# First loads on one queue, a small extra read of the modulation weights, and the last store on another engine

## The chip, the core and the metric

The kernel runs on one core of one Trainium2 chip. The core has five engines with instruction queues of their own: TensorE (PE in the profile; its weight loads are listed apart as PEld), VectorE (DVE), ScalarE (ACT), GpSimd (POOL) and SyncE (SP), which here only issues transfers. Transfers run on 16 DMA engines that all queues share. Transfers issued by SyncE appear as queue q1 in the profile, those issued by ScalarE as q10. The metric is device time in microseconds (us) of one execution, given as the median of several runs.

## What is computed

A transformer block with adaptive layer norm: a condition vector c gives six modulation rows, a local dilated attention (32 heads of 16, a window of 8 positions with a step of 2) is added to x, and then a token-mixing MLP over the 2048 positions. B = 1, S = 2048, D = 512, F = 1792; all inputs are bfloat16.

```python
mod = (silu(c) @ w_mod).reshape(1, 6, 1, 512)        # w_mod: 512 x 3072
sa, ca, ga, sb, cb, gb = (mod[:, i] for i in range(6))
h = layernorm(x) * (1 + ca) + sa
x = x + ga * A(h, wqkv, wo)                          # local dilated attention
h = layernorm(x) * (1 + cb) + sb
x = x + gb * B(h, w1, b1, w2, b2)                    # B normalizes again, then
# u = gelu(einsum('bsd,sf->bdf', h, w1) + b1);  y = einsum('bdf,fs->bds', u, w2) + b2;  transposed back
```

## The kernel before, in words

**How the order is made.** The kernel first builds a graph of named operations, each with the engines it may run on and what it reads and writes. A long string, `ORDER`, lists all the names in the order in which they are emitted; `name:2` gives a PSUM slot (there are four, `ps0` to `ps3`) and `name:v`, `name:a` or `name:g` the engine. `schedule` checks that nothing comes before what it depends on. Each engine then runs its own operations in that order. Places of operations of different engines relative to each other have no meaning beyond their data. Since all operations are recorded through one helper, the profile gives line 184 for nearly everything, and tiles must be used to tell them apart.

**How transfers are issued.** `dma` (line 346) issues on SyncE unless told `"act"`. Completion is counted on eight counters that are used in turn by all transfers, in the order in which they are emitted: a transfer's issue waits until the transfer eight places earlier, which had the same counter, has landed. SyncE runs its issues strictly in order, so a waiting issue holds those behind it.

**The start.** x has 2048 rows in 16 tiles of 128 (`xx`), in four chunks of four tiles. The transfers are named: `ld_c` (c, ScalarE), `ld_x00` and `ld_x02` (tiles 0, 1 and 2, 3 of chunk 0, 256 KB each), `ld_wmodA` and `ld_wmodB` (the first 1024 columns of `w_mod`, its upper and lower 256 rows, 512 KB each, into tile `vD0`; called wmodA and wmodB below), `ld_w1a`, `ld_w1b` (the key weights `w_k`, 256 KB each), `ld_x1a`, `ld_x1b`, `ld_x2`, `ld_x3` (the other chunks), `ld_w0` (`w_q`), `ld_w2` (`w_v`), then the other modulation weights (`ld_wmod5` and so on, into `wst`) and `woq`. Before the change SyncE issues x00, x02, wmodB, w1a, x1a, w1b, x1b, x2, w0, w2, x3 in this order, and ScalarE issues c and then wmodA, ahead of its table load.

The first computations of chunk 0 are: `cps` and the silu of c (ScalarE and VectorE, `silu_exp`, `silu_dve`), the statistics `ln1s0` to `ln1s3` of the four tiles (VectorE takes 0, 2 and 3, ScalarE takes 1), `rstd1_0_0` and `rstd1_0_2` on ScalarE, the normalization `ln1n0` to `ln1n3` into `n_sb` on VectorE, 16 transposes on TensorE in four groups (`tr0_00`, `tr0_10`, `tr0_02`, `tr0_12`), and the modulation columns. For these, `modcols0` (from wmodA) and `modcols1` (from wmodB) are 16 products each with one column; `modcols_h` copies the first half (`mchalf`), and `modcols_cp` adds the second half, into `sacol` and `a1col`. With these, `hT0_0` to `hT0_3` scale and shift the transposed tiles: ScalarE does `hT0_0`, VectorE the other three. Then come the projections, keys first: `qkvk0_0` (its second half, `qkvk0_0b`, needs all of hT), `qkvk0_2`, `qkvk0_1`, then the queries (`qkvq0_...`, from `w_q`). `warm0` to `warm4` are products of a constant with itself whose result is never read; `WARM` gives their counts. `warm4` stands between the last transposes and `qkvk0_0`.

**What follows.** For each chunk: products of q and k on VectorE (`qk`, 128 x 4096), their reduction on TensorE (`red`), softmax, products with the shifted v (`pv`, VectorE; `pvacc`, TensorE), the output projection (`wo`), two more normalizations (`t`, `aff`, `h3`). The first MLP product runs in two halves (`mlp1_0_...` over the positions of chunks 0 and 1, `mlp1_1_...` over the others), joined by `gadd`, `gelu` and `gbm`. The second MLP product (`mlp2_...`) runs over 16 tiles of output rows; `fin` adds the residual on VectorE, and `st_out` stores. Tile 15 is split into columns 0 to 383 and 384 to 511; its second part, `st_out15_384`, is the last store, right behind `st_out14_0` on SyncE.

Of the kernel before, what the change touches and what calls it, by code (L numbers as in the profile page):

```python
# [32 lines left out]
qkvq0_2:3 ln1n7:v evk0_2:a evq0_0:a rstd1_2_0 qk0_1 evq0_2:a tr1_10:2 tr1_00:1 ld_w2 ld_x3 ld_wmod5 ld_wmod3 ld_wo0
ld_wmod2 ld_wo2 ld_wo1 khalo1 ld_wmod4 qkvv0_0:0 qk0_0 hT1_0:a hT1_1:a hT1_2:a hT1_3:a qk0_3 qk0_2 evv0_0:a qkvv0_2:3
qkvq1_0:1 evv0_2:a ln1s14:a vd0_111 vd0_010 vd0_031 vd0_100 vd0_101 vd0_021 vd0_030 vd0_001 vd0_020 vd0_011 vd0_000
vd0_130 vd0_120 vhalo1 evq1_0:a nb1_2_0 qkvk1_0:2 red0_0:0 evk1_0:a red0_1 ln1s12:v ln1s13:v ln1n11:g ln1n10:g red0_2
red0_3 qk1_1 qkvq1_2:3 ln1s15:a rstd1_3_0 ln1n8:a evq1_2:a ln1n9:a qkvk1_2:1 max0 qk1_0 sub0 qkvv1_0:2 evk1_2:a exp0
tr2_10:3 evv1_0:a sum0 rb0 tr2_00:1 qkvv1_2:2 hT2_1:a qk1_3 smul0 qk1_2 nb1_3_0 khalo2 vd0_110 vd0_131 vd0_121 hT2_0:a
hT2_3:a a2_0:0 a2ev0:a red1_0:3 modrows:0 pv0_0 pv0_1 hT2_2:a ln1n14:a evv1_2:a mrow_ev ln1n12:a ln1n13:a ln1n15:a
qkvq2_0:1 red1_1 red1_2 red1_3 pvacc0_0:2 max1 pvacc0_1 evq2_0:a tr3_00:0 pv0_2 pv0_3 sub1 hT3_0:a vd1_011 vd1_020  # L40
ld_wo3 bc0 vd1_031 qkvk2_0:1 exp1 vd1_010 vd1_030 vd1_000 vd1_021 vd1_001 sum1 hT3_2:a oev0_1:a qkvv2_0:0 rb1 evk2_0:a
smul1 pvacc0_2:2 evv2_0:a vd1_130 vd1_110 vd1_120 vd1_100 vd1_101 vd1_111 vd1_131 vd1_121 pvacc0_3 gmul a2_1:3
oev0_3:a tr3_10:1 qk2_1 hT3_1:a a2ev1:a wo3:0 wo0:2 wo2:3 x1ev3:a hT3_3:a x1ev0:a x1ev2:a x1sq0 wo1:0 pv1_0 pv1_1
qkvq2_2:1 pvacc1_0:2 qk2_0 x1ev1:a x1sq3 x1sq2 x1sq1 pvacc1_1 qkvv2_2:3 qkvk2_2:0 rstd2_0_0 evq2_2:a nb2_0_0 pv1_2
qkvq3_0:1 t1:a t3:a t2:v pv1_3 oev1_1:a evk2_2:a evq3_0:a t0:a bc3 bc1 bc2 ld_w1_0_0 vhalo2 khalo3 ld_w1_0_2 ld_b2
ld_w1_0_3 pvacc1_2:2 red2_0:0 qk2_3 pvacc1_3 qkvk3_0:1 oev1_3:a evv2_2:a aff0_0 wo6:2 evk3_0:a wo4:3 x1ev6:a vd2_110
vd2_001 vhalo3 vd2_031 ld_b1 vd2_120 ld_w1_0_1 vd2_000 wo5:1 qk2_2 x1sq6 x1ev4:a wo7:2 x1sq4 x1ev5:a red2_1 ln3s0_1:v
x1ev7:a qk3_1 x1sq5 x1sq7 qkvk3_2:3 red2_2 rstd2_1_0 red2_3 evk3_2:a nb2_1_0 qkvq3_2:1 t5:a t7:g t6:g t4:g ln3s0_3:a
ln3s0_2:v max2 ln3s0_0:v sub2 qkvv3_2:2 exp2 rstd3_0_0 evq3_2:a biascols:3 sum2 qkvv3_0:1 aff1_0 nb3_0_0 evv3_2:a
h3_0:a h3_1:g h3_2:g ln3s1_1:a rb2 ln3s1_0:a evv3_0:a ln3s1_3:v biascols_cp ln3s1_2:v h3_3:v qk3_0 smul2 qk3_2  # L50
mlp1_0_30_0:3 mlp1_0_10_0:2 mlp1_0_31_0 a2_2:0 mlp1_0_11_0 rstd3_1_0 vd2_021 vd2_111 vd2_030 vd2_020 vd2_011 vd2_121
ld_w1_0_6 vd2_010 vd2_131 vd2_130 vd3_020 vd3_030 vd3_010 vd2_100 a2ev2:a red3_0:1 red3_1 nb3_1_0 qk3_3 red3_2
mlp1_0_00_0:0 mlp1_0_01_0 h3_4:v h3_5:a h3_6:a h3_7:a red3_3 pv2_0 mlp1_0_11_4 mlp1_0_31_4 mlp1_0_10_4 mlp1_0_01_4
max3 park0_1:a pv2_1 sub3 pvacc2_0:2 exp3 mlp1_0_30_4 pv2_2 vd2_101 vd3_000 vd3_031 vd3_001 vd3_011 vd3_110 vd3_021
vd3_121 vd3_100 vd3_120 vd3_130 ld_w1_0_4 vd3_131 vd3_111 vd3_101 sum3 mlp1_0_00_4 pvacc2_1 park0_3:a rb3 oev2_1:a
smul3 mlp1_0_60_0:3 pv2_3 a2_3:1 mlp1_0_61_0 pvacc2_2:2 a2ev3:a pvacc2_3 pv3_0 mlp1_0_60_4 mlp1_0_61_4 oev2_3:a wo10:1
wo8:2 pv3_1 park0_6:a x1ev10:a x1sq10 park0_0:a wo11:3 x1ev8:v wo9:1 x1ev11:v pvacc3_0:2 ld_w1_1_0 ld_w1_0_5 ld_w1_1_1
ld_w2_4 ld_w1_1_5 ld_w1_1_3 x1ev9:v pvacc3_1 pv3_2 mlp1_0_20_0:0 mlp1_0_21_0 mlp1_0_40_0:3 mlp1_0_21_4 mlp1_0_20_4
mlp1_0_40_4 pvacc3_2:1 x1sq8 x1sq11 x1sq9 rstd2_2_0 nb2_2_0 pv3_3 t8:v t10:a t9:a t11:a aff2_0 pvacc3_3 oev3_1:a
park0_2:a oev3_3:a ln3s2_3:a ln3s2_1:v ln3s2_2:v ln3s2_0:v mlp1_0_41_0 mlp1_0_41_4 wo12:2 wo13:0 park0_4:a x1ev12:v  # L60
rstd3_2_0 wo14:1 wo15:3 mlp1_0_50_0:2 x1ev13:v x1sq12 nb3_2_0 x1sq13 h3_8:a rstd2_3_0 x1ev14:v x1ev15:v h3_10:g
h3_11:g mlp1_0_51_0 mlp1_0_51_4 mlp1_0_50_4 h3_9:v nb2_3_0 t13:v t12:v x1sq15 x1sq14 aff3_0 rstd2_3_2 park0_5:a
# [5 lines left out]
mlp1_1_41_4 gelu5 gelu4 gbm7 gadd5 gbm5 gbm6 gbm2 gelu10 gelu11 gbm10 gadd4 gbm4 gbm11 mlp1_1_60_0:2 mlp1_1_61_0
mlp1_1_61_4 mlp1_1_60_4 gelu8 gelu9 gbm8 gbm9 mlp2_3_0_0:3 mlp2_1_0_0:0 gadd6 gelu13 gelu12 xb3 gbm12 gbm13
mlp2_3_12_0 mlp2_2_0_0:1 fin3_0 xb2 st_out3_0 xb0 xb1 mlp2_2_12_0 xb7 mlp2_0_0_0:2 fin2_0 st_out2_0 ld_w2_2  # L70
mlp2_1_12_0 mlp2_0_12_0 mlp2_7_0_0:3 fin0_0 mlp2_7_12_0 mlp2_6_0_0:1 fin7_0 xb6 st_out7_0 st_out0_0 mlp2_6_12_0
mlp2_11_0_0:2 fin6_0 xb4 st_out6_0 ld_w2_7 mlp2_5_0_0:3 xb10 xb11 fin1_0 st_out1_0 mlp2_10_0_0:1 xb5 mlp2_11_12_0
# [894 lines left out]
```

## Time and profile before

| what | value |
|---|---|
| median of 3 runs | 198.81 us (198.49 to 199.16) |
| the profiled execution: its own time | 198.58 us |
| its span, first to last instruction | 196.4 us |
| TensorE busy | 190.3 us (97%), 1290 products |
| VectorE busy | 154.3 us (79%) |
| ScalarE busy | 124.0 us (63%) |
| GpSimd busy | 11.9 us (6%) |
| moved by DMA | 33.58 MB, of it 32.85 MB on SyncE's queue and 0.53 MB on ScalarE's |

The profile shows one execution. Its 2.2 us beyond the span lie before the first and after the last instruction. Busy shares are averages over stages: TensorE's products are pipelined and their ends are modelled, so 97% doesn't mean that it ran at its peak. In the profile's 40 slices each digit is a busy share in tenths for 4.9 us. In its timeline a line is: start (us from the span's start), duration, engine, operation, tiles written and read, shape, count, and in brackets the idle time before it and what ended it. In the chain of waits a line is: start, duration, what. In the list of transfers the last figure is the time from issue to landing in us. The trace also has a record of every DMA packet (start, duration, size and queue); where a number comes from there, the text says packet records.

### The profile page before, as it was taken

What the parts mean: (1) busy time and instruction counts of PE and PEld (TensorE: products, weight loads), DVE (VectorE), ACT (ScalarE), POOL (GpSimd) and SP (SyncE); (2) the same over time, 40 slices, a digit from 0 to 9 for tenths busy, and PEclk for the clock granted to TensorE, in tenths of its full rate; (3) what the DMA queues carried; (4) which work ended last, traced back from release to release, by engine and by line L of the source; (5) the groups of instructions that cost most, each with busy time, mean ns of one, the idle gap of its engine ahead of it and who ended that gap; (6) DMA issues with size and microseconds to landing.
All of it is one profiled execution on the core that took longest, in us unless ns stands there. A gap on an engine that the chain in (4) does not pass through costs nothing.

```text
span 196.4 us, 3401 instructions
## 1 busy us (share of the span) xinstructions
PE 190.3 (97%) x1290; PEld 88.8 (45%) x1290; DVE 154.3 (79%) x200; ACT 124.0 (63%) x241; POOL 11.9 (6%) x41
## 2 busy tenths in 40 slices
PE   7999999899999999999999999999999999999994
...
DVE  1799999999999999999999998827984547142463
...
PEclk9999999999999999999999999999999999999999
DMA  6999999346990995299599989999000164511112
GB/s 195 364 348 326 244 189 167 94 137 157 158 232 11 239 230 164 76 222 190 130 217 290 292 240 292 291 294 243 3 0 0 57 201 129 150 44 36 57 57 76
DMA packets 45347, 33.58 MB, mean 171 GB/s; under 512 B 5396, under 2 KB 42772, under 8 KB 45332
## 3 DMA queue, kind: packets, MB, share of 16 engines
q1 hardware_dynamic: 45052, 32.85, 67.5%
q10 hardware_dynamic: 280, 0.53, 0.8%
q8 instruction: 10, 0.16, 0.4%
...
## 4 chain that ended last, share of the span: by engine, by line
PE 58%; ACT 23%; DVE 11%; issue 5%; DMA 2%; SPq 0%; DVEq 0%; ACTq 0%
PE ps L184 58%; ACT junk L184 4%; ACT hTb L184 3%; DVE pvb L184 3%; ACT n_sb L184 2%; ACT v_c L184 2%; ACT q_sb L184 2%; DMA xx<-in_A_x_dram 2%; ACT k_c L184 2%; DVE prod L184 2%; DVE st L184 2%; DVE h L184 2%; ACT xx L184 1%; ACT a2sb L184 1%; ACT ee L184 1%
## 5 line engine op out<-in xcount | busy, mean ns | idle before, releaser
L184 DVE TENSOR_TENSOR pvb<-a2sb,vD 128x4096 bf16<-128x4096 bf16 x16 | 36.2, 2289 | 0.4 <-issue 0.2
L184 PE MATMUL ps<-h,wst 128*128 128x512 bf16 x128 | 29.3, 380 | 0.0
L184 DVE TENSOR_TENSOR prod<-q_sb,k_c 128x4096 bf16<-128x4096 bf16 x9 | 20.6, 2296 | 0.1
L184 PE MATMUL ps<-gT,vD 128*128 128x512 bf16 x84 | 19.1, 379 | 0.0
L184 PEld LDWEIGHTS <-wst 128*128 128x128 bf16 x128 | 12.1, 98 | 15.5 <-issue 1.7
L184 DVE TENSOR_TENSOR k_c<-ps,k_c 128x512 bf16<-128x512 f32 (+2 forms) x9 | 5.6, 630 | 13.4 <-PE ps L184 13.4
L184 PE MATMUL ps<-woq,o_sb 128*128 128x512 bf16 x64 | 15.7, 379 | 0.0
L184 PE MATMUL ps<-hTb,w_v 128*128 128x512 bf16 x64 | 15.0, 380 | 0.4 <-ACT q_sb L184 0.4
L184 PEld LDWEIGHTS <-w_q 128*128 128x128 bf16 x96 | 10.1, 109 | 11.2 <-issue 1.7
L184 PE MATMUL ps<-hTb,w_q 128*128 128x512 bf16 x64 | 15.0, 381 | 0.0
L184 PE MATMUL ps<-hTb,w_k 128*128 128x512 bf16 x64 | 15.0, 380 | 0.0
L184 PEld LDWEIGHTS <-o_sb 128*128 128x128 bf16 x106 | 9.7, 98 | 10.3 <-ACT o_sb L184 0.4
L184 DVE TENSOR_TENSOR q_sb<-ps,q_sb 128x512 bf16<-128x512 f32 x8 | 5.4, 687 | 11.1 <-PE ps L184 11.1
L184 PEld LDWEIGHTS <-vD 128*128 128x128 bf16 x116 | 9.3, 97 | 10.1
L184 PE MATMUL ps<-gT,pvb 128*128 128x512 bf16 x56 | 12.9, 379 | 0.0
L184 PEld LDWEIGHTS <-w_k 128*128 128x128 bf16 x80 | 8.7, 111 | 8.9 <-issue 0.8
L184 PE MATMUL ps<-gT,prod 128*128 128x512 bf16 x56 | 12.2, 379 | 0.0
L184 PEld LDWEIGHTS <-w_v 128*128 128x128 bf16 x80 | 8.3, 110 | 8.6 <-issue 1.7
L184 ACT ACTIVATE junk<-xx,su 128x512 bf16<-128x512 bf16 x16 | 11.6, 726 | 0.3
L184 DVE BATCH_NORM_STATS2 st<-xx 128x6 f32<-128x512 bf16 x11 | 7.4, 674 | 4.6 <-DMA xx<-in_A_x_dram 4.6
L184 ACT ACTIVATE gT<-n_sb,b1col 128x512 bf16<-128x512 f32 x8 | 5.4, 714 | 8.8 <-DVE n_sb L184 8.8
L184 ACT ACTIVATE hTb<-ps,sacol,a1col 128x512 bf16<-128x512 bf16 x13 | 9.6, 780 | 1.4 <-PE ps L184 1.4
(111 smaller groups left out, 315.6 us busy)
## 6 DMA issues: line engine op xcount, KB each, us to landing
...
wst<-in_B_w_dram SPq DMA_DIRECT2D x8, 512.0 KB, 6.2
...
wst<-in_w_mod_dram SPq DMA_DIRECT2D x4, 512.0 KB, 9.4
...
xx<-in_A_x_dram SPq DMA_DIRECT2D x4, 256.0 KB, 3.5
xx<-in_A_x_dram SPq DMA_DIRECT2D x2, 512.0 KB, 8.0
```

The source lines that it names most:

```text
L184: r = fn(*a, **k)
```

## The change

Five things are changed in the code:

- `ld_wmodA` is issued by SyncE, as third transfer, between `ld_x02` and `ld_wmodB`. The rest of the order of SyncE's first loads stays.
- A new transfer, `ld_touch`, takes its place on ScalarE: it reads the first 32 columns (64 B) of rows 0, 8, 16, ... 504 of `w_mod` into a tile of 64 x 32 that nothing reads.
- The last store, `st_out15_384`, is issued by ScalarE.
- The last count in `WARM` is 5, not 6.
- `ORDER` is written anew. Engine by engine, this changes little beyond the above. TensorE: `modcols1` now stands ahead of all the transposes (before: behind `tr0_00`); in the second half of the first MLP product, `mlp1_1_00_0` stands ahead of `mlp1_1_11_0`, `mlp1_1_20_4` ahead of `mlp1_1_50_4`, and `mlp1_1_41_4` ahead of `mlp1_1_40_4`. VectorE: `modcols_h` ahead of `ln1n3`; `t8` ahead of `pv3_3`; `gadd5` ahead of `gbm7`. SyncE: `ld_w2_0` (into `prod0`) goes behind `ld_w1_1_4`, `ld_w2_5` and `ld_w2_3`. GpSimd: nothing.

Since the touch is one more transfer at the start, the transfers behind it use the next counter: the issue of `ld_w1b` now waits for c, `ld_x1b` for x00, `ld_x2` for the touch, `ld_w0` for x02, `ld_w2` for wmodA and `ld_x3` for wmodB (before: `ld_x1b` for c, `ld_x2` for x00, and the others as now).

```diff
 ORDER = """
-consts ld_c ld_x00 consts2 warm0:0 ld_x02 ld_wmodA act_table ld_wmodB ld_w1a ld_x1a cps:1 warm1:2 ld_w1b silu_exp
-ln1s0:v ld_x1b ln1s1:a ld_x2 silu_dve halo0 ld_w0 warm2:3 ln1s2:v rstd1_0_0 ln1s3:v modcols0:0 nb1_0_0 ln1n0:v warm3:1
-rstd1_0_2 ln1n1:v nb1_0_2 ln1n2:v tr0_00:2 ln1n3:v modcols1 modcols_h tr0_10:3 tr0_02 modcols_cp tr0_12 sc_rep hT0_1:v
+consts ld_c ld_x00 consts2 warm0:0 ld_touch ld_x02 act_table ld_wmodA ld_wmodB ld_w1a cps:1 warm1:2 ld_x1a silu_exp
+ln1s0:v ld_w1b ln1s1:a ld_x1b silu_dve ln1s2:v halo0 ld_x2 warm2:3 ld_w0 ln1s3:v rstd1_0_0 modcols0:0 rstd1_0_2 ld_w2
+nb1_0_0 ln1n0:v warm3:1 ln1n1:v nb1_0_2 ln1n2:v modcols1 modcols_h ln1n3:v ld_x3 tr0_00:2 tr0_10:3 modcols_cp tr0_02
...
-    WARM=(4, 4, 4, 4, 6),
+    WARM=(4, 4, 4, 4, 5),
...
+    touch = T([D // 8, 32], BF, "touch")
...
     dma(c_t[:], c[0].rearrange("(t p) -> t p", p=P), 1024, [], ["c_t"], "ld_c", "act")
+    dma(touch[:], w_mod.rearrange("(a b) n -> a b n", b=8)[:, 0, 0:32], 4096, [], ["touch"], "ld_touch", "act")
...
-    dma(wmodA[:, 0:2, :], wmod_view[:, 0:2, 0:2 * D], 2 * D * P * 2 * 2, [], vdk[0][4:], "ld_wmodA", "act")
+    dma(wmodA[:, 0:2, :], wmod_view[:, 0:2, 0:2 * D], 2 * D * P * 2 * 2, [], vdk[0][4:], "ld_wmodA")
...
                 dma(out_flat[st * P:(st + 1) * P, c0:c1], ostage[:, c0:c1], P * nc_ * 2, ok[1:] or ok, [("out", st, c0)],
-                    f"st_out{st}_{c0}")
+                    f"st_out{st}_{c0}", "act" if st == NST - 1 and c1 == D else "sp")
```

More of the change, by code (lines that the diff above doesn't have):

```diff
@@ L33 @@
[L33 to L62, printed above, removed]
@@ L68 @@
[L68 to L72, printed above, removed]
@@ new lines @@
+sc_rep tr0_12 hT0_0:a warm4:1 hT0_1:v ld_wmod5 ln1s4:a hT0_3:v qkvk0_0:0 hT0_2:v ln1s6:v qkvk0_0b ld_wmod3 ln1s7:a
+qkvk0_2:1 ln1s5:v ln1s9:v ld_wo0 rstd1_1_0 ld_wmod2 qkvk0_1:3 ln1s10:v evk0_0:a qkvq0_1:2 nb1_1_0 ln1s8:v evk0_1:a
+ln1n4:g ld_wo2 ln1n5:a qkvq0_0:0 ld_wo1 ln1s11:v ln1n6:g evq0_1:a qkvq0_2:3 ln1n7:v evk0_2:a qk0_1 evq0_0:a khalo1
+rstd1_2_0 tr1_10:2 ld_wmod4 evq0_2:a tr1_00:1 qkvv0_0:0 qk0_0 hT1_0:a hT1_1:a qkvv0_2:3 hT1_2:a qk0_3 hT1_3:a evv0_0:a
+qkvq1_0:1 evv0_2:a qk0_2 ln1s14:a vd0_111 qkvk1_0:2 vd0_010 vd0_031 evq1_0:a nb1_2_0 ln1s12:v red0_0:0 vd0_100
@@ new lines @@
+ln1n11:g evk1_0:a red0_1 vd0_101 ln1s13:v ln1n10:g red0_2 ln1s15:a vd0_021 red0_3 qk1_1 qkvq1_2:3 vd0_030 vd0_001
+rstd1_3_0 vd0_020 ln1n8:a qkvk1_2:1 max0 vd0_011 evq1_2:a vd0_000 qk1_0 vd0_130 ln1n9:a sub0 vd0_120 qkvv1_0:2
+evk1_2:a vhalo1 exp0 khalo2 qk1_3 vd0_110 tr2_10:3 evv1_0:a sum0 vd0_131 tr2_00:1 rb0 qkvv1_2:2 vd0_121 hT2_1:a smul0
+hT2_0:a qk1_2 hT2_3:a a2_0:0 a2ev0:a red1_0:3 nb1_3_0 hT2_2:a modrows:0 pv0_0 ln1n14:a qkvq2_0:1 evv1_2:a mrow_ev
+pv0_1 vd1_011 ln1n12:a red1_1 vd1_020 red1_2 ln1n13:a ld_wo3 red1_3 ln1n15:a bc0 pvacc0_0:2 max1 pvacc0_1 vd1_031
@@ new lines @@
+evq2_0:a tr3_00:0 vd1_010 pv0_2 sub1 hT3_0:a vd1_030 qkvk2_0:1 exp1 vd1_000 vd1_021 hT3_2:a vd1_001 pv0_3 sum1
+oev0_1:a qkvv2_0:0 vd1_130 rb1 vd1_110 evk2_0:a vd1_120 smul1 pvacc0_2:2 vd1_100 evv2_0:a pvacc0_3 gmul vd1_101 a2_1:3
+oev0_3:a tr3_10:1 vd1_111 qk2_1 vd1_131 hT3_1:a wo3:0 a2ev1:a vd1_121 wo0:2 x1ev3:a bc3 pv1_0 hT3_3:a wo2:3 bc1
+x1ev0:a bc2 wo1:0 x1ev2:a pv1_1 ld_w1_0_0 x1sq0 qkvq2_2:1 x1ev1:a vhalo2 x1sq3 pvacc1_0:2 qk2_0 x1sq2 pvacc1_1 x1sq1
+qkvv2_2:3 rstd2_0_0 evq2_2:a nb2_0_0 pv1_2 qkvk2_2:0 t1:a t3:a oev1_1:a qkvq3_0:1 t2:v pv1_3 evk2_2:a pvacc1_2:2
@@ new lines @@
+khalo3 evq3_0:a red2_0:0 ld_w1_0_2 qk2_3 pvacc1_3 ld_b2 t0:a qkvk3_0:1 ld_w1_0_3 oev1_3:a evv2_2:a aff0_0 wo6:2
+evk3_0:a vd2_110 wo4:3 vd2_001 x1ev6:a vhalo3 x1sq6 wo5:1 qk2_2 vd2_031 x1ev4:a ld_b1 wo7:2 x1sq4 vd2_120 x1ev5:a
+ld_w1_0_1 red2_1 ln3s0_1:v vd2_000 x1ev7:a qkvk3_2:3 qk3_1 x1sq5 vd2_021 vd2_111 x1sq7 vd2_030 red2_2 rstd2_1_0 red2_3
+evk3_2:a nb2_1_0 ln3s0_2:v qkvq3_2:1 vd2_020 t7:g t5:a vd2_011 max2 t4:g ln3s0_3:a vd2_121 t6:g ln3s0_0:v sub2
+qkvv3_2:2 aff1_0 exp2 rstd3_0_0 biascols:3 sum2 evq3_2:a nb3_0_0 ln3s1_3:v evv3_2:a h3_1:g qkvv3_0:1 biascols_cp
@@ new lines @@
+h3_2:g h3_0:a ln3s1_2:v ln3s1_1:a h3_3:v qk3_0 ld_w1_0_6 mlp1_0_30_0:3 vd2_010 rb2 mlp1_0_10_0:2 vd2_131 ln3s1_0:a
+vd2_130 mlp1_0_31_0 smul2 qk3_2 a2_2:0 evv3_0:a mlp1_0_11_0 rstd3_1_0 vd3_020 red3_0:1 a2ev2:a vd3_030 red3_1 nb3_1_0
+qk3_3 vd3_010 red3_2 h3_5:a mlp1_0_00_0:0 vd2_100 h3_6:a vd2_101 mlp1_0_01_0 h3_7:a vd3_000 h3_4:v red3_3 pv2_0
+vd3_031 mlp1_0_11_4 vd3_001 mlp1_0_31_4 vd3_011 max3 mlp1_0_10_4 vd3_110 vd3_021 mlp1_0_01_4 park0_1:a pv2_1 sub3
+pvacc2_0:2 exp3 mlp1_0_30_4 pv2_2 vd3_121 sum3 park0_3:a vd3_100 mlp1_0_00_4 vd3_120 rb3 pvacc2_1 vd3_130
@@ new lines @@
+mlp1_0_60_0:3 smul3 oev2_1:a ld_w1_0_4 pv2_3 a2_3:1 vd3_131 mlp1_0_61_0 vd3_111 a2ev3:a vd3_101 pvacc2_2:2 ld_w1_1_0
+pvacc2_3 pv3_0 mlp1_0_60_4 ld_w1_0_5 oev2_3:a mlp1_0_61_4 wo10:1 pv3_1 park0_6:a wo8:2 x1ev10:a wo11:3 x1sq10
+ld_w1_1_1 x1ev8:v park0_0:a wo9:1 x1ev11:v x1sq8 pvacc3_0:2 ld_w2_4 x1ev9:v pvacc3_1 x1sq11 pv3_2 mlp1_0_20_0:0 x1sq9
+mlp1_0_21_0 rstd2_2_0 mlp1_0_40_0:3 ld_w1_1_5 nb2_2_0 t8:v t10:a mlp1_0_21_4 pv3_3 t9:a mlp1_0_20_4 t11:a ld_w1_1_3
+mlp1_0_40_4 oev3_1:a aff2_0 pvacc3_2:1 park0_2:a pvacc3_3 mlp1_0_41_0 oev3_3:a mlp1_0_41_4 ln3s2_1:v ln3s2_3:a wo12:2
@@ new lines @@
+ln3s2_2:v ld_w1_1_6 ld_w2_6 wo13:0 park0_4:a ln3s2_0:v wo14:1 x1ev12:v rstd3_2_0 x1ev13:v wo15:3 x1sq12 nb3_2_0
+ld_w1_1_2 x1ev14:v x1sq13 mlp1_0_50_0:2 h3_10:g x1ev15:v h3_8:a h3_11:g mlp1_0_51_0 rstd2_3_0 h3_9:v ld_w2_1
+mlp1_0_51_4 x1sq15 nb2_3_0 t13:v t12:v x1sq14 mlp1_0_50_4 aff3_0 rstd2_3_2 mlp1_1_50_0:0 park0_5:a nb2_3_2 mlp1_1_51_0
+t15:v ld_w1_1_4 ln3s3_0:a t14:v mlp1_1_10_0:1 aff3_2 mlp1_1_00_0:3 ln3s3_1:a ln3s3_3:v ld_w2_5 mlp1_1_11_0 ln3s3_2:v
+mlp1_1_01_0 rstd3_3_0 nb3_3_0 rstd3_3_2 mlp1_1_30_0:2 h3_12:v h3_13:a nb3_3_2 h3_15:v h3_14:v mlp1_1_31_0 ld_w2_3
@@ new lines @@
+mlp1_1_10_4 mlp1_1_31_4 mlp1_1_00_4 mlp1_1_01_4 ld_w2_0 mlp1_1_11_4 gadd0 mlp1_1_30_4 gadd1 gelu1 mlp1_1_20_0:3
+mlp1_1_21_0 gelu3 gelu2 mlp1_1_21_4 gbm3 gbm1 gelu0 gadd3 mlp1_1_20_4 mlp1_1_50_4 gbm0 gelu7 gadd2 mlp1_1_51_4 gelu6
+mlp1_1_40_0:1 gelu5 gadd5 gelu4 mlp1_1_41_0 gbm7 gelu10 mlp1_1_41_4 gbm5 gbm6 gelu11 gbm2 mlp1_1_40_4 gbm10
+mlp1_1_60_0:2 gadd4 mlp1_1_61_0 gbm4 gelu8 mlp1_1_61_4 gbm11 gelu9 gbm8 mlp1_1_60_4 gbm9 mlp2_3_0_0:3 gadd6 xb3 gelu13
+gelu12 mlp2_1_0_0:0 gbm12 gbm13 mlp2_3_12_0 mlp2_2_0_0:1 fin3_0 xb2 st_out3_0 xb0 xb1 mlp2_2_12_0 xb7 mlp2_0_0_0:2
```

13 lines of the change are left out of this document (4 added, 9 removed).

## The prediction

> **What bounds the kernel now.** I read the slices first, then the chain that ended last in order of time, then the timeline and transfers of the first 14 us and of the end.
>
> ```profile
> PE   7999999899999999999999999999999999999994
> DVE  1799999999999999999999998827984547142463
> PEclk9999999999999999999999999999999999999999
> DMA  6999999346990995299599989999000164511112
> GB/s 195 364 348 326 244 189 167 94 137 157 158 232 11 239 230 164 76 222 190 130 217 290 292 240 292 291 294 243 3 0 0 57 201 129 150 44 36 57 57 76
> ```
>
> TensorE (PE) is busy from start to end at full clock, VectorE (DVE) nearly so up to slice 24, and the first three slices (4.9 us each) run at 326 to 364 GB/s after the start: the loads are one unbroken stream.
>
> ```profile
> 1.30 4.24 DMA xx<-in_A_x_dram
> ...
> 8.90 0.16 DVE sacol L184
> ...
> 9.23 0.78 ACT hTb L184
> ...
> 83.48 108.79 PE ps L184 x637
> ```
>
> The chain enters by a transfer of x, goes through the modulation columns into the first hT, and then over ScalarE (ACT) and DVE to 83.48, from where PE alone sets the end. The kernel has no slack to swallow a later start, and an earlier one can come through.
>
> ```profile
> 5.56 0.69 DVE L184 BATCH_NORM_STATS2 st<-xx 128x6 f32<-128x512 bf16 x1 [0.95 <-DMA xx<-in_A_x_dram]
> ...
> 5.93 0.67 PEld L184 LDWEIGHTS <-vD 128*128 128x128 bf16 x16
> ...
> 7.18 1.42 DVE L184 TENSOR_SCALAR n_sb<-xx,mv,rs 128x512 bf16<-128x512 bf16 x4
> ...
> 8.07 0.51 PEld L184 LDWEIGHTS <-vD 128*128 128x128 bf16 x16
> ...
> 8.50 0.68 PEld L184 LDWEIGHTS <-n_sb 128*128 128x128 bf16 x12
> ...
> 9.39 1.45 DVE L184 TENSOR_SCALAR hTb<-ps,a1col,sacol 128x512 bf16<-128x512 bf16 x3
> ...
> 10.49 3.62 PE L184 MATMUL ps<-hTb,w_k 128*128 128x512 bf16 x16
> ...
> 13.72 3.35 PEld L184 LDWEIGHTS <-w_q 128*128 128x128 bf16 x16
> ```
>
> Here x02 (issued 1.30) keeps DVE idle until 5.56, modcols1 (second vD load) sits behind the first transposes, and the key projection starts at 10.49. The transfers of these windows:
>
> ```profile
> xx<-in_A_x_dram SPq DMA_DIRECT2D x1, 256.0 KB, 4.2
> ...
> vD<-in_w_mod_dram SPq DMA_DIRECT2D x1, 512.0 KB, 5.6
> ...
> w_q<-in_A_wqkv_dram SPq DMA_DIRECT2D x1, 512.0 KB, 7.7
> ```
>
> Issue plus the last column: x02 lands at 1.30 + 4.2 = 5.5, wmodB at 1.80 + 5.6 = 7.4, w_q at 5.76 + 7.7 = 13.46.
>
> **The change part by part.** *x02 alone ahead.* wmodA left ScalarE at 1.39 and shared the engines with x02. On one queue x02 follows x00, which landed at 0.80 + 2.8 = 3.6. Its 262 kB at 0.36 MB/us (as in slice 2) take 0.73, so it lands at 4.3. DVE is free after silu at 4.61 and starts the statistics then, 0.95 sooner. The rescaling into n_sb needs ScalarE's rs, which ends at 6.17, so it starts at 6.2 instead of 7.18 and ends, with mchalf's 0.17 now inside it, at 7.8 instead of 8.6.
>
> *wmodA on SyncE.* It adds one issue (0.47, spaced 0.51) ahead of wmodB, w1a, x1a and w1b, each 0.51 later. They are queued ahead of their data: in the packet records wmodB's first packet moves at 5.06, 3.3 after its issue, and w1b's at 8.0. Cost nothing; without that backlog, 0.51. The bytes ahead of wmodA's and wmodB's ends are the same, so they land at 5.8 and 7.4 as before.
>
> *modcols1 ahead of the transposes.* Now it waits for wmodB alone. After wmodA's landing at 5.8 PE loaded at 5.93, so here at 7.55, and the 16 loads end at 8.06. All 16 transposes follow at 0.68/12 = 0.057 each, so the last load ends at 8.98 against 9.18: 0.20 gained. DVE's first hT goes from 9.39 to 9.19. ScalarE's needs only 12 transposes and goes from 9.23 to about 8.96.
>
> *One warm-up matmul fewer.* Six ran from 9.19 to 10.49, so 0.22 each. The projection could start at 10.49 - 0.20 - 0.22 = 10.07, but its second half needs DVE's third hT, which ends at 9.19 + 1.45 = 10.64 against a former place at 10.94. PE gains about 0.22; the cut only makes room for the 0.20.
>
> *The touch.* ScalarE issues it in wmodA's old place (0.42), ahead of the table load at 1.84: no change there. 64 rows of 64 B, four packets per engine. No operation of before is like it. The nearest row is c's, whose 256 B packets took 15 ns. What it may save: 26 packets of wmodA and wmodB took over 0.10 us, up to 0.40, against a median of 0.084, nearly all in the first half of each. wmodB's packets span 1.61 us; at w1a's rate (0.73 for half the bytes) they would span 1.46. x02 with wmodA span 2.30; the same way 2.18. So at most 0.15 + 0.12 = 0.27 on wmodB's landing, if these slow reads are first reads of a stretch. At the other end the same reads stall earlier, beside x00 and x02: 0, or a loss (third rival). I take 0.14, half, because two queues at once still moved 0.79 MB in 2.30 us (342 GB/s), so stalls of one can be covered by the other. Front: 0.20 + 0.14 = 0.34. The touch also takes a completion slot: x2's issue (4.5 before, now about 5.0) waits for it, with w0, w2 and x3 behind. x2's first packet moves at 9.5, so it may land 4 us late before that matters.
>
> [...]
>
> *What is late next.* w_q is usable some 0.1 after 13.46, and PE takes it at 13.72 now: room of 0.16, or 0.30 with the stream 0.14 earlier. That caps the front at 0.30. After it w_v (6.18 + 8.8 = 15.0) is due at 18.2; DVE and ScalarE run without gaps, so 0.30 reaches 83.48 and the end.
>
> *Later reorderings.* t8 goes ahead of pv3_3 on DVE: 0.41 later, to 110.7, used by PE in the second half of a group that starts at 111.13. mlp1_1_00 goes ahead of mlp1_1_11 with the weights issued at 98.9, two dozen us before; gadd5 goes ahead of gbm7, and PE never waits there. The load into prod0 drops behind three others on SyncE, but the stream is empty in slices 28 to 30 (137 to 152 us) and prod0's weights are first read near 148. All nothing.
>
> *The last store.*
>
> ```profile
> 194.04 0.38 SPq L184 DMA_DIRECT2D out_dram<-k_c  x1
> ...
> out_dram<-k_c SPq DMA_DIRECT2D x1, 32.0 KB, 1.5
> ```
>
> DVE's last sum ends at 193.81, but SyncE issues at 194.04, behind st_out14 (193.62). ScalarE, idle since 148, can issue at about 193.85 and lands at 195.35 instead of 195.54. st_out14 lands at 193.62 + 1.7 = 195.32, so it isn't the next limit by much. Gain 0.19; bounds 0 (a slower wake of ScalarE) and 0.22.
>
> **Sum.** 0.30 + 0.19 = 0.49 off the profiled execution: span 196.4 to 195.9, its time 198.58 to 198.09. The median lies 0.23 above that execution, so 198.3.
>
> **Rivals.** *Only the tail comes through.* The slow reads of w_mod now lie alone on SyncE's queue, where no x02 covers them, and the touch does not warm them: it fetches 64 B of every eighth row, and nothing shows that a neighbour's read is then quicker. wmodB then lands up to 0.27 later, which eats the 0.20; 0.19 remains: 198.6. For it: w1a, first of its own tensor, had no packet over 0.084, so "first read" is not proven. Against: x00's slow packets lie at its start.
>
> *The slowest engine.* A landing is set by the slowest of 16 engines, and 0.27 is a mean. Should one engine have met two of the slow packets (0.39 and 0.36), it lost 0.6. If the touch takes that away, wmodB lands near 6.9, and the front is limited by n_sb at 7.8 and the transposes behind it: the first hT moves up by as much as 0.7, w_q with the stream. 0.7 + 0.19 = 0.9: 197.9. Against: the mean rate hardly dipped.
>
> *Slower: the touch blocks.* Its four packets per engine hit four separated stretches, each as slow as wmodA's slowest (0.39), one after the other, in front of x02 and wmodA: up to 4 x 0.39 = 1.56 on each engine. It decides once wmodB lands over 0.4 late (0.20 + 0.19 gone); with three such reads uncovered, 1.17 late, the time is 198.8 + 0.78 = 199.6. For it: x00's 256 packets span 1.18 us where 0.73 would do, so a slow read does hold its engine. Against: the 342 GB/s with both queues. [...]
>
> **How the numbers follow.** Forecast 0.45, only the tail 0.20, slowest engine 0.25, blocking 0.10. A measurement of this kernel tells about 0.3% (0.6 us) from no change, so faster means below 198.21. Nearly all of the slowest-engine case, 0.4 of the forecast (which lies just above the line) and little of the tail case make 0.45; blocking gives 0.09 slower; 0.46 is left for the same. The range runs from 197.75 (0.9 with some spread of the runs, 198.49 to 199.16 before) to 199.0, a touch that costs half of its bound or a front that is lost; without the blocking case it would end at 198.8.
>
> **What would show it.** x02 lands near 4.3 and DVE's second statistics start near 4.6, right if so; modcols1 loads start at 7.4 to 7.55 (forecast), by 7.1 (slowest engine), at 8 or later (blocking). The key projection's second half starts 0.2 to 0.4 before 10.94, w_q's first load at 13.4, PE's last stretch starts near 83.2. The last store is issued by ScalarE within 0.06 of DVE's end. It is wrong if wmodB lands after 7.8, if w_q holds PE at 13.7, or if PE's last stretch starts at 83.5 in spite of an earlier start.

## The result, and the profile after the change

The changed kernel takes 201.22 us (median of 5 runs, 199.59 to 201.83), the kernel before on the same chip 198.74 (5 runs, 198.49 to 199.16): a ratio of 1.012, 95% interval 1.0092 to 1.0148. It is slower by 2.5 us, outside the predicted range. In the runs the clock granted to TensorE differs: its mean was 1.0 in the run of 199.59 and 0.991 in the other four. The ratios in this text leave out runs more than 1.5% above the fastest of their kernel; now and then the kernel before has such a run too (3 of 19 in the last comparison, 201.24 to 203.09, clock 0.983 to 0.991).

The profiled execution is one of 201.22 us, with a span of 199.0. Its slices:

```profile
PE   7599999999999999989999999999999999999994
DVE  2479999999999999999999998918884646142563
PEclk9889999999999999999999999999999999999999
DMA  5999969916991599099499999999000163601112
GB/s 152 328 351 335 243 160 169 155 61 190 171 231 37 125 220 272 15 232 212 129 203 260 293 232 301 291 292 280 10 0 0 56 184 108 182 29 50 56 56 76
```

Two lines changed where before there were only nines: PE in the second slice (4.9 to 9.8 us), and the granted clock in the second and third. From the fourth slice on, little is different. The chain that ended last, in order of time (start, duration, what):

```profile
1.80 6.10 DMA vD<-in_w_mod_dram
7.95 3.84 PE ps L184 x48
11.82 0.78 ACT hTb L184
...
195.50 0.90 DVE k_c L184 x2
```

It no longer enters by x (before: 1.30 + 4.24), but by wmodA, issued at 1.80 and landed at 7.9. ScalarE's first hT starts at 11.82 against 9.23, 2.59 late; the products from which PE alone sets the end start at 86.08 against 83.48, 2.60 late; DVE's last sums start at 195.50 against 192.91, again 2.59 late. So the whole loss is made in the first 12 us, and nothing behind gives any of it back or adds to it, none of the later reorderings either (on GpSimd, too, one pair is exchanged: `t4` now stands ahead of `t6`). The timeline of that stretch:

```profile
4.49 0.69 DVE L184 BATCH_NORM_STATS2 st<-xx 128x6 f32<-128x512 bf16 x1
...
6.21 1.06 DVE L184 TENSOR_SCALAR n_sb<-xx,mv,rs 128x512 bf16<-128x512 bf16 x3
...
7.95 0.49 PEld L184 LDWEIGHTS <-vD 128*128 128x128 bf16 x16 [2.58 <-DMA vD<-in_w_mod_dram]
7.95 0.58 PE L184 MATMUL ps<-sc,vD 128*128 128x1 bf16 x16 [2.09 <-DMA vD<-in_w_mod_dram]
...
8.39 1.87 PE L184 MATMUL ps<-ident 128*128 128x512 bf16 x4
...
10.05 0.52 PEld L184 LDWEIGHTS <-vD 128*128 128x128 bf16 x15 [0.28 <-issue]
...
12.04 1.45 DVE L184 TENSOR_SCALAR hTb<-ps,a1col,sacol 128x512 bf16<-128x512 bf16 x3 [0.58 <-PE ps L184]
...
12.92 3.38 PE L184 MATMUL ps<-hTb,w_k 128*128 128x512 bf16 x13
```

DVE's side went as planned: the second statistics start at 4.49 and the rescaling at 6.21. But PE then stands idle for 2.09 us until wmodA is there, the four warm-ups behind it start 0.42 apart instead of 0.22, and modcols1 comes at 10.05. The transfers (out<-in, queue, count, size, median us from issue to landing):

```profile
vD<-in_w_mod_dram SPq DMA_DIRECT2D x2, 512.0 KB, 6.5
...
touch<-in_w_mod_dram ACTq DMA_DIRECT2D x1, 4.0 KB, 3.1
```

The 6.5 is the mean of wmodA's 6.1 and, so, 6.9 for wmodB, which was issued at 2.31 and landed at 9.2 (before 7.4). Finally windows of 1 us: the window, its length, the busy shares of PE, PEld, DVE, ACT and POOL with their instructions, then the granted clock, the DMA share and GB/s. Before:

```profile
4.00:5.00 1.00, 1.00 (x3) 0.30 (x2) 0.58 (x3) 0.97 (x4) 0.89 (x11) 1.00 1.06 406
5.00:6.00 1.00, 1.00 (x5) 0.45 (x4) 0.44 (x1) 0.97 (x5) 0.00 (x0) 1.00 1.00 344
```

After:

```profile
4.00:5.00 1.00, 1.00 (x4) 0.36 (x3) 0.97 (x4) 0.97 (x4) 0.89 (x11) 1.00 0.60 184
5.00:6.00 1.00, 0.86 (x4) 0.20 (x2) 0.93 (x4) 0.97 (x5) 0.00 (x0) 1.00 0.94 201
...
8.00:9.00 1.00, 1.00 (x18) 0.65 (x19) 0.00 (x0) 0.00 (x0) 0.00 (x0) 0.52 1.04 371
9.00:10.00 1.00, 1.00 (x3) 0.30 (x2) 0.00 (x0) 0.00 (x0) 0.00 (x0) 0.50 1.10 385
10.00:11.00 1.00, 1.00 (x22) 0.95 (x21) 0.30 (x2) 0.00 (x0) 0.00 (x0) 0.50 1.10 362
11.00:12.00 1.00, 1.00 (x15) 0.94 (x13) 0.46 (x4) 0.18 (x1) 0.00 (x0) 0.78 1.10 347
```

Between 4 and 6 us the transfers move 184 and 201 GB/s where they moved 406 and 344; that is 365 KB less, about 1 us of the stream. From 4 to 5 the DMA engines are busy 60% of the time only; from 5 to 6 they are busy 94% of it and still move little: single packets take long (14 of the table's below over 0.3 us, up to 0.94). Then, from 8.03 to 11.45, the granted clock is halved.

The packet records show the slow reads. The table is on the first 512 packets of 2 KB (wmodA and wmodB together), whose median duration is 0.084 us; the last two kernels in it are those of the first experiment:

```
kernel                          over 0.1   over 0.3   longest     sum of what lies over 0.084
before                              26         6      0.40 us      3.5 us
after                               45        14      0.94 us     11.7 us
wmodA on SyncE, no touch            52        25      1.02 us     15.6 us
wmodA on ScalarE, no touch          16         3      0.37 us      1.9 us
```

The slow packets are unevenly spread: wmodA's parts on the 16 DMA engines landed within 0.3 us of each other before (5.45 to 5.75), and within 2.4 us after (5.46 to 7.9). The product waits for the last: it starts at 7.95, and the last part landed at 7.91.

### The profile page after: what moved, and what is told of

The parts are those of the page before. It is cut to its first block, busy times and chain, and to the rows that moved or that the text cites. A ratio compares the mean times of both kernels' runs of the same rounds, so it can differ in the third digit from the quotient of the medians.

```text
span 199.0 us, 3378 instructions
## 1 busy us (share of the span) xinstructions
PE 189.5 (95%) x1267; PEld 89.2 (45%) x1289; DVE 154.0 (77%) x200; ACT 123.9 (62%) x241; POOL 11.9 (6%) x41
## 4 chain that ended last, share of the span: by engine, by line
PE 58%; ACT 19%; DMA 8%; DVE 7%; SPq 4%; issue 4%; DVEq 0%; ACTq 0%
PE ps L184 58%; ACT junk L184 4%; SPq L184 4%; DMA vD<-in_w_mod_dram 3%; ACT hTb L184 3%; DMA vD<-v_c 3%; DMA wst<-in_B_w_dram 2%; ACT n_sb L184 2%; ACT k_c L184 2%; ACT v_c L184 2%; ACT q_sb L184 2%; DVE h L184 2%; DVE st L184 1%; ACT xx L184 1%; DVE pvb L184 1%
## 5 line engine op out<-in xcount | busy, mean ns | idle before, releaser
L184 PE MATMUL ps<-h,wst 128*128 128x512 bf16 x123 | 28.5, 379 | 0.3 <-issue 0.2
```

The lines of the kernel that those rows point to most:

```text
L184: r = fn(*a, **k)
```

## The experiments

All times are medians with their range, and every ratio is to runs of the kernel before on the same chip (198.73 beside experiments 1 to 4, 6 and the first of 7, 198.75 beside the others). Experiments 1, 6 and the first of 2 ran on one chip, the others on a second. Where the edits are shown, the lines of `ORDER` and of the tile `touch` that only follow from them are left out. "Key projection" is its first product; before the change it starts at 10.49.

**1. Which part of the change does it?** First the change without the touch, then the same with wmodA back on ScalarE.

```diff
-    dma(touch[:], w_mod.rearrange("(a b) n -> a b n", b=8)[:, 0, 0:32], 4096, [], ["touch"], "ld_touch", "act")
```

> The changed kernel without the touch; wmodA stays on SyncE's queue. Theory 1 (uncovered reads: the slow first reads of w_mod stall SyncE's queue, which has no second queue beside it; the touch is idle talk): wmodA still lands at 7.5 to 8.0 us and modcols0 starts near 7.9; time 199.6 to 201.5. Theory 2 (collision: the touch's 64 small reads meet wmodA's first reads in the same stretches and make them slower): wmodA lands by 6.2, x02 at 4.3, modcols0 starts by 6.3; time 198.2 to 198.7.

```diff
-    dma(touch[:], w_mod.rearrange("(a b) n -> a b n", b=8)[:, 0, 0:32], 4096, [], ["touch"], "ld_touch", "act")
...
-    dma(wmodA[:, 0:2, :], wmod_view[:, 0:2, 0:2 * D], 2 * D * P * 2 * 2, [], vdk[0][4:], "ld_wmodA")
+    dma(wmodA[:, 0:2, :], wmod_view[:, 0:2, 0:2 * D], 2 * D * P * 2 * 2, [], vdk[0][4:], "ld_wmodA", "act")
```

> The changed kernel with wmodA back on ScalarE and without the touch: what is left of the change is modcols1 ahead of the transposes, one warm-up matmul fewer, the later reorderings and the last store. Both theories: wmodA lands at 5.75 and x02 at 5.5 as before the change; time 198.3 to 198.7 (0.2 from the last store, 0.2 from the start). If it is slower than 199.2, a part of the change that neither theory names is at work (the last store, the shorter warm-up).

Without the touch: 200.21 (199.65 to 201.85), ratio 1.010 (1.0069 to 1.0132). With wmodA on ScalarE as well: 198.87 (198.39 to 199.90), 1.0014 (0.9998 to 1.0029). The intervals don't meet, so the queue of this one transfer makes the difference (198.87 is a little above the 198.3 to 198.7 expected). The timeline of w_mod's weight loads with wmodA on SyncE,

```profile
7.54 0.47 PEld L184 LDWEIGHTS <-vD 128*128 128x128 bf16 x16 [1.49 <-DMA vD<-in_w_mod_dram]
...
8.89 0.47 PEld L184 LDWEIGHTS <-vD 128*128 128x128 bf16 x16 [0.41 <-DMA vD<-in_w_mod_dram]
```

and on ScalarE:

```profile
5.95 0.47 PEld L184 LDWEIGHTS <-vD 128*128 128x128 bf16 x16 [0.33 <-DMA vD<-in_w_mod_dram]
...
7.57 0.47 PEld L184 LDWEIGHTS <-vD 128*128 128x128 bf16 x16 [0.67 <-DMA vD<-in_w_mod_dram]
```

wmodA is there 1.6 us and wmodB 1.3 us later when SyncE issues both. From 4 to 5 us the transfers move 393 GB/s with both queues at work, the DMA engines busy 90% of the time or more, and with wmodA on SyncE only 127, the engines busy 77% of it:

```profile
4.00:5.00 1.00, 1.00 (x3) 0.30 (x2) 0.97 (x4) 0.97 (x4) 0.89 (x11) 1.00 0.77 127
```

What is left of the change with wmodA on ScalarE can't be told from the kernel before.

**2. The touch ahead of wmodA on ScalarE's queue**, with w_mod's rows, and then with as many rows of x in their place. The first edit is against the changed kernel, the second against the first.

```diff
-consts ld_c ld_x00 consts2 warm0:0 ld_touch ld_x02 act_table ld_wmodA ld_wmodB ld_w1a cps:1 warm1:2 ld_x1a silu_exp
+consts ld_c ld_x00 consts2 warm0:0 ld_touch ld_x02 ld_wmodA act_table ld_wmodB ld_w1a cps:1 warm1:2 ld_x1a silu_exp
...
-    dma(wmodA[:, 0:2, :], wmod_view[:, 0:2, 0:2 * D], 2 * D * P * 2 * 2, [], vdk[0][4:], "ld_wmodA")
+    dma(wmodA[:, 0:2, :], wmod_view[:, 0:2, 0:2 * D], 2 * D * P * 2 * 2, [], vdk[0][4:], "ld_wmodA", "act")
```

> The changed kernel with wmodA back on ScalarE's queue, behind the touch. Theory 1: two queues run side by side again, so wmodA lands at 5.7 to 6.3 whatever the touch does, x02 near 5.5; time 198.2 to 198.7. Theory 2: the touch still runs just ahead of wmodA, so wmodA lands at 7 or later and the time is 199.6 to 201.5.

```diff
-    dma(touch[:], w_mod.rearrange("(a b) n -> a b n", b=8)[:, 0, 0:32], 4096, [], ["touch"], "ld_touch", "act")
+    dma(touch[:], x_flat[0:D, :].rearrange("(a b) n -> a b n", b=8)[:, 0, 0:32], 4096, [], ["touch"], "ld_touch", "act")
```

> wmodA on ScalarE behind a touch that reads 64 x 64 B of x (every eighth of its first 512 rows) instead of w_mod: same number, size and place of small packets. The same kernel with the touch on w_mod took 203.5 us, wmodA at 9.7. Theory W (the harm comes from reading w_mod cold at scattered places): wmodA lands at 5.6 to 6.3, time 198.4 to 199.1. Theory S (64 small packets ahead of wmodA on its queue do the harm, whatever they read): wmodA at 8 or later, time 201 or more.

The first took 203.52 (203.34 to 203.74), ratio 1.0245 (1.0229 to 1.026), more than either theory had expected; the second took 203.84 (202.89 to 204.02), 1.0251 (1.0211 to 1.029). Against wmodA on ScalarE without a touch (198.87), 64 packets of 64 B cost more than 4 us, with rows of w_mod as with rows of x. In all eight runs the mean granted clock was 0.983 to 0.992, so a part of this is the clock's. In the first of the two:

```profile
1.96 0.60 ACTq L184 DMA_DIRECT2D vD<-in_w_mod_dram  x1
...
10.24 0.37 SPq L184 DMA_DIRECT2D w_v<-in_A_wqkv_dram  x1
10.26 0.47 PEld L184 LDWEIGHTS <-vD 128*128 128x128 bf16 x16 [4.21 <-DMA vD<-in_w_mod_dram]
```

The issue for w_v waits for wmodA, and both it and the first weight load follow right behind wmodA's landing at 10.22. (The 9.7 that the second expectation gives for wmodA is the landing of wmodB.) wmodA leaves 0.55 later than without the touch (1.41), its first packet moves 1.70 later (5.16 against 3.46), and it lands 4.3 later (10.22 against 5.91). wmodB's packets, on SyncE's queue, went ahead of it: they start at 3.72 instead of 5.13. The touch's own packets took at most 0.011 us each, but they are spread from 3.66 to 4.67. Ten of the 16 engines had wmodA by 7.3, the others only at 8.8 to 10.22. Why the queue is held up behind the touch is open.

**3. Does the touch make the reads behind it quicker?** The touch ahead of c, wmodA on SyncE.

```diff
-consts ld_c ld_x00 consts2 warm0:0 ld_touch ld_x02 act_table ld_wmodA ld_wmodB ld_w1a cps:1 warm1:2 ld_x1a silu_exp
+consts ld_touch ld_c ld_x00 consts2 warm0:0 ld_x02 act_table ld_wmodA ld_wmodB ld_w1a cps:1 warm1:2 ld_x1a silu_exp
```

> The changed kernel with the touch as ScalarE's first transfer, ahead of c (issue at 0.8 instead of 1.4 us); wmodA stays on SyncE. Theory A (a read of every eighth row does take the slow first reads on itself, if it has run before wmodA's first packet): few packets of w_mod over 0.3 us (before the change 6, in the changed kernel 14), wmodA lands by 6.2, time 198.2 to 198.8. Theory B (it warms nothing; the reads of w_mod stay slow on SyncE's queue): ten or more packets over 0.3 us, wmodA at 7 or later, time 199.6 to 201.5.

It took 200.49 (200.13 to 201.14), ratio 1.0095 (1.0059 to 1.0132): as without a touch. In the changed kernel the touch's packets ran from 3.40 to 3.90, and wmodA's began at 3.51: the touch came with the reads that it should precede. Here it was done by 3.24 and wmodA began at 3.68, yet 26 packets took over 0.3 us (25 without a touch). Reading 64 B of every eighth row didn't make the reads behind it quicker.

**4. Other work on the other queue.** x02 on ScalarE and wmodA on SyncE, so that two queues are again at work.

```diff
-            f"ld_x0{i}")
+            f"ld_x0{i}", "act" if i else "sp")
```

> No touch; the roles of the queues are exchanged: x02 goes to ScalarE's queue, wmodA stays on SyncE's, now right behind x00. Theory P (w_mod's first reads are quick if any other queue moves data beside them): wmodA lands at 5.6 to 6.3, as before the change, few packets over 0.3 us; time 198.3 to 199.0. Theory H (they are quick only if wmodA heads a queue of its own, so that its reads are asked for while the engines still move x00): behind x00 in one queue wmodA lands at 6.8 or later with ten or more packets over 0.3 us; time 199.4 to 201.

It took 199.21 (198.84 to 202.09), ratio 1.0031 (1.0001 to 1.0061), between the ranges of the two theories. This is closer to wmodA on ScalarE (1.0014) than to both on SyncE (1.010). But the profiled execution is one of the slowest, at 201.15: in it 17 packets took over 0.3 us, wmodA landed at 7.20 and x02 at 8.24. Of these 17, 13 start before x02's first packet moves at 3.47, while SyncE's queue is still alone with wmodA. It speaks for the second queue as cover, and does not prove it; the landings in the quicker runs aren't known.

**5. Is it the first read of these rows?** wmodA and wmodB on SyncE, without a touch, reading rows of x: ones that x00 and x02 have just read, or ones that nothing has read.

```diff
-    dma(wmodA[:, 0:2, :], wmod_view[:, 0:2, 0:2 * D], 2 * D * P * 2 * 2, [], vdk[0][4:], "ld_wmodA")
-    dma(wmodA[:, 2:4, :], wmod_view[:, 2:4, 0:2 * D], 2 * D * P * 2 * 2, [], vdk[0][:4], "ld_wmodB")
+    dma(wmodA[:, 0:2, :], x_flat[0:512, :].rearrange("(k p two) n -> p k (two n)", k=2, two=2), 2 * D * P * 2 * 2, [], vdk[0][4:], "ld_wmodA")
+    dma(wmodA[:, 2:4, :], x_flat[0:512, :].rearrange("(k p two) n -> p k (two n)", k=2, two=2), 2 * D * P * 2 * 2, [], vdk[0][:4], "ld_wmodB")
```

> The change without the touch, wmodA and wmodB on SyncE's queue, but both read the first 512 KB of x, which x00 and x02 have just read, in rows of 2 KB, instead of w_mod (so the modulation columns, and the output, come from other data; sizes and work stay). In the version that reads w_mod they landed at 7.5 and 8.85, with 25 packets above 0.3 us, and the time was 200.2. Theory F (the first read of a stretch of a DRAM tensor is slow): landings by 6.0 and 7.5, fewer than 6 packets above 0.3 us, 198.2 to 198.9. Theory Q (it is one queue alone that is slow, whatever it reads): landings at 7.3 or later and 8.6 or later, 200 to 200.5. Theory R (rows 6 KB apart are slow): as F here.

In the other kernel the rows are `x_flat[1024:1536, :]` and `x_flat[1536:2048, :]`.

> The same, but wmodA reads rows 1024 to 1535 of x and wmodB rows 1536 to 2047, which nothing has read by then (again the modulation columns come from other data). Theory F: as slow as w_mod, wmodA at 7 or later, more than 15 packets above 0.3 us, 199.9 to 200.5. Theory Q: the same, 200 to 200.5. Theory R (stride of w_mod's rows): quick, landings by 6.0 and 7.5, 198.2 to 198.9.

Rows not read before took 200.46 (199.95 to 201.72), ratio 1.011 (1.0081 to 1.0139), with 25 packets over 0.3 us, as with w_mod. So neither w_mod nor the 6 KB between its rows is the cause. Rows just read have a ratio of 1.0054 (1.0031 to 1.0076). But their eight runs spread from 198.97 to 203.23 (median 200.12), three of them above 202.7, and the profiled execution is one of these three: 13 packets over 0.3 us, and wmodA landed at 8.32. How wmodA landed in the other five isn't known. A repeated read is better in most runs, yet not free of the stalls: theory F explains a part at most; the rest goes with the queue, as theory Q has it, or is open.

**6. Does the halved clock cost something of its own?** Ten more warm-ups where PE would stand idle.

```diff
-    WARM=(4, 4, 4, 4, 5),
+    WARM=(4, 4, 14, 4, 5),
```

> The changed kernel with 14 instead of 4 matmuls in the third warm-up, 10 x 0.216 = 2.2 us more, which covers TensorE's idle time from 5.8 to 7.9 us. If the halved clock from 8.0 to 11.4 us comes from that idle time, the clock stays at 1.0, the key projection starts near 11.3 instead of 12.9, and the time is 199.4 to 199.9 with wmodA still landing near 7.9. If the halved clock has another cause, it stays at 0.991 on average and the time at 200.9 to 201.9.

It took 200.63 (200.23 to 201.42), ratio 1.0104 (1.0076 to 1.0131), with a clock of 0.998 to 1.0 in all four runs. That is more than the 199.4 to 199.9 expected: in its profiled execution wmodA landed at 8.26 and wmodB at 9.68, later still than in the changed kernel. But the clock stayed up:

```profile
8.00:9.00 1.00, 1.00 (x18) 0.64 (x17) 0.00 (x0) 0.00 (x0) 0.00 (x0) 1.00 1.06 352
9.00:10.00 1.00, 1.00 (x16) 0.52 (x13) 0.00 (x0) 0.00 (x0) 0.00 (x0) 1.00 1.08 382
```

and the key projection began at 12.51 against 12.92 in the changed kernel. So the halved clock (0.991 on average in four of the changed kernel's five runs) goes with PE's idle time of 2.09 us; with that covered, the late landing remains.

**7. wmodA later, and earlier.** Two other places on ScalarE's queue without a touch: behind the table load in the order, and ahead of c. The edits are against the kernel of experiment 1 with wmodA on ScalarE.

```diff
-consts ld_c ld_x00 consts2 warm0:0 ld_x02 ld_wmodA act_table ld_wmodB ld_w1a cps:1 warm1:2 ld_x1a silu_exp
+consts ld_c ld_x00 consts2 warm0:0 ld_x02 act_table ld_wmodA ld_wmodB ld_w1a cps:1 warm1:2 ld_x1a silu_exp
```

> No touch; wmodA on ScalarE's queue, but issued behind the table load, at about 2.7 us instead of 1.4, when x02 is half through. Theory P (two queues side by side): it still has wmodB's traffic of SyncE beside it; it starts 0.5 to 1.0 later and lands at 6.3 to 7.0 with few packets over 0.3 us; time 198.8 to 199.4. Theory H (an early request, while x00 moves, hides the slow reads): ten or more packets over 0.3 us, wmodA at 7.2 or later; time 199.5 to 201. The table load moves no earlier work: ScalarE's first activation starts at 3.46 and the load ends by then.

```diff
-consts ld_c ld_x00 consts2 warm0:0 ld_x02 ld_wmodA act_table ld_wmodB ld_w1a cps:1 warm1:2 ld_x1a silu_exp
+consts ld_wmodA ld_c ld_x00 consts2 warm0:0 ld_x02 act_table ld_wmodB ld_w1a cps:1 warm1:2 ld_x1a silu_exp
```

> No touch; wmodA on ScalarE's queue and ahead of c, so issued at 0.8 beside x00 instead of 1.4 beside x02; the rest of the change is kept. With wmodA at 1.4 this was 198.87 (same). Theory C (slow packets of w_mod cost nothing while the other queue has bytes to move, and the sooner wmodA starts, the longer it is covered): wmodA by 5.6, wmodB by 7.4, time 198.3 to 198.8, at best a little ahead of before. Rival: x00 and c land later by what wmodA takes from them (c then behind wmodA's packets, silu and modcols0 late), 199.2 or more.

The first said nothing on its question: the issue was still made at 1.44, beside the table load (1.41) and not behind it. Its time was 200.23 (198.66 to 202.84), ratio 1.0048 (1.0002 to 1.0094), and its ten runs were five of 198.66 to 199.10 (clock 0.998 to 1.0) and five of 201.37 to 202.84 (0.983 to 0.991), though it is nearly the program whose ten runs above, on the other chip, were all at 0.999 or more. That fits a landing of wmodA that varies between runs of one program, but it isn't shown: the one profiled execution is of 198.75, and there wmodA landed at 6.28. The second took 201.21 (200.64 to 201.79), ratio 1.0136 (1.0116 to 1.0156), though w_mod came as quickly as hoped, with 4 packets over 0.3 us:

```profile
4.94 0.69 DVE L184 BATCH_NORM_STATS2 st<-xx 128x6 f32<-128x512 bf16 x1 [4.94 <-DMA xx<-in_A_x_dram]
5.33 0.10 PEld L184 LDWEIGHTS <-c_t 4*128 4x128 bf16 x1 [2.92 <-DMA c_t<-in_c_dram]
```

x00 is 1.3 us later (3.6 in the changed kernel) and c 2.1 us (3.24 there), and with c the silu and both modulation columns: the rival was right.

**8. The last store alone** on ScalarE, in the kernel before.

```diff
-                    f"st_out{st}_{c0}")
+                    f"st_out{st}_{c0}", "act" if st == NST - 1 and c1 == D else "sp")
```

> The kernel before with the last store on ScalarE's queue and nothing else. Prediction's term: 0.19 (bounds 0 and 0.22), so 198.55 against 198.73, ratio 0.999. Rival: ScalarE's issue and landing take longer than SyncE's and give it back, 198.7 to 198.9.

It took 198.45 (198.18 to 201.05), ratio 1.0003 (0.9977 to 1.0029): no difference that can be told. The end in its timeline:

```profile
193.09 0.90 DVE L184 TENSOR_TENSOR k_c<-ps,k_c 128x512 bf16<-128x512 f32 x2
...
194.02 0.37 ACTq L184 DMA_DIRECT2D out_dram<-k_c  x1
```

and the last store in its list of transfers:

```profile
out_dram<-k_c ACTq DMA_DIRECT2D x1, 32.0 KB, 1.7
```

The issue follows DVE's end (193.99) by 0.03 instead of 0.23, but landing takes 1.7 instead of 1.5. By the landing records the last one is 1.70 behind DVE's end, against 1.74 before.

## Why the prediction was wrong, step by step

**The step that failed** is "wmodA on SyncE": "Cost nothing", because "the bytes ahead of wmodA's and wmodB's ends are the same, so they land at 5.8 and 7.4 as before". They landed at 7.9 and 9.2, and at 7.5 and 8.85 without the touch. The step counted bytes against a mean rate, 0.36 MB/us, and took it as given that the stream keeps it. Before, wmodA's reads shared the 16 engines with x02's, which came from another queue. Behind x02 on one queue, the excess of wmodA's and wmodB's packets over 0.084 us went from 3.5 us in all to 11.7 (15.6 without the touch). That the queue does this is shown by the pair in experiment 1; why reads are slower on one queue is not. wmodB after 7.8, which the prediction had named as a sign that it is wrong, is what was seen. The trace of before had the warning in it: the two queues together moved 342 GB/s in spite of the slow packets, which was read only as a limit to what the touch could gain.

**The "only the tail" rival named this mechanism**, slow reads that no x02 covers and a touch that helps nothing, and both came true, though the cover itself isn't proven. Its size was wrong: "up to 0.27", taken from the stalls seen while x02's packets ran beside them, and spread evenly over 16 engines. Without x02's beside them there were more and longer ones (14 over 0.3 us, up to 0.94, against 6 up to 0.40), wmodA's parts landed up to 2.4 us apart, and the last engine decides; wmodB was 1.8 late. The "slowest engine" rival saw that a mean hides the worst engine, but put it on the side of the gain. The blocking rival had the sign and the closest time (199.6), not the mechanism: the touch's packets took at most 0.011 us, and the loss is there without it.

**A second loss was not foreseen.** No step asked what PE does while it waits for wmodA. It stood idle for 2.09 us, and the clock was at half from about 8.0 to 11.45. With wmodA on ScalarE and the rest of the change, modcols1 loads at 7.57 and the key projection starts at 10.19. wmodB 1.70 later (9.2 against 7.5) would put modcols1 at 9.27; at half clock the four warm-ups ahead of it hold it until 10.05, 0.78 more, and from there to the projection it is 2.87 instead of 2.62, 0.25 more. That splits the 2.73 between 10.19 and 12.92 into 1.70 for the landing and 1.03 for the clock. The ten more warm-ups bear this out: from wmodB's landing to the projection it is 3.70 in the changed kernel (9.22 to 12.92) and 2.83 with them at full clock (9.68 to 12.51), so the clock is worth about 0.9.

**The touch**, put at a gain of 0.14: none. In its place in the changed kernel a cost of its own isn't resolved (1.012 with it, 1.010 without, intervals that overlap); ahead of wmodA on one queue it costs more than 4 us, though its 64 packets took at most 0.011 us each.

**x02 alone ahead** was right up to the rescaling: x02 landed at 4.27 (forecast 4.3), the statistics started at 4.49 (4.61) and the rescaling at 6.21 (6.2). It is worth nothing while w_mod decides. The end of the rescaling, forecast for 7.8, could not hold even with modcols1 loading at 7.55 as forecast, as the next lines show.

**modcols1 ahead, one warm-up fewer** were right in part where wmodB was not late: in the kernel with wmodA on ScalarE modcols1 loads at 7.57 (forecast 7.55) and the projection starts 0.30 sooner, at 10.19. But w_q's first load there starts at 13.62 against 13.72 before: of the 0.30 only 0.10 passes.

```profile
8.16 0.17 DVE L184 COPY mchalf<-ps 128x8 f32<-128x8 f32 x1 [0.30 <-PE ps L184]
...
8.25 0.41 DVE L184 TENSOR_SCALAR n_sb<-xx,mv,rs 128x512 bf16<-128x512 bf16 x1
...
8.71 0.39 PEld L184 LDWEIGHTS <-n_sb 128*128 128x128 bf16 x7 [0.23 <-DVE n_sb L184]
...
9.31 1.45 DVE L184 TENSOR_SCALAR hTb<-ps,a1col,sacol 128x512 bf16<-128x512 bf16 x3 [0.39 <-PE ps L184]
...
10.81 2.71 PEld L184 LDWEIGHTS <-w_k 128*128 128x128 bf16 x13 [0.29 <-issue]
```

The copy mchalf starts 0.04 behind the last product of modcols1 (7.57 + 0.55 = 8.12), as in the kernel before (8.70 behind 8.66), and it now stands ahead of the last tile's rescaling. That ends at 8.66, the last seven transposes wait 0.23 for it, and DVE's first hT starts 0.08 sooner than before (9.31) instead of 0.20. DVE's third hT ends at 9.31 + 1.45 = 10.76, and the second half of the projection starts behind it, at 10.81 against 10.92. The prediction had named this wait for the third hT, but put it at 10.64. The cap that it set, w_q, didn't hold PE here: w_q landed at 13.55, and PE goes from the keys to the queries without a gap.

**The last store**, put at 0.19, moved the last landing by 0.04: issue came 0.20 sooner, landing took 0.16 longer. That landing takes as long from either queue had been assumed without a word.

So of the 0.49 about 0.14 existed (0.10 ahead of w_q, 0.04 at the store), below what this measurement can tell, and no version tried is measurably faster than the kernel before.
